# Third unit's values in one burst, first scores four matmuls later, another order of products in one step

## The chip, the cores and the metric

The kernel runs on one core of one Trainium2 chip. The metric is the time of one execution in device microseconds (us). Times in the text that look like 38.54 are positions in the profiled execution, counted from its first instruction.

## What is computed

Windowed causal attention with a window of 64 positions, and then a feed-forward block with a ReLU gate, on 4608 tokens:

```python
# attention: 8 batches, 8 heads, 576 positions, head dimension 64
scores = (q @ k.T) / sqrt(64); masked to 0 <= i - j < 64; softmax
x = (attn @ v)                 # transposed to (4608, 512)
# feed-forward: 512 -> 1536 -> 512
out = (maximum(x @ w_gate, 0) * (x @ w_val)) @ w_out
```

Inputs and output are float32; the kernel multiplies in float16 and adds up in float32.

## The kernel before

**Tiles and stages.** The tokens are taken in tiles `t`: 384, 192, 448 and then seven of 512. For a tile the attention is made (scores, exponential, mask, values, division, transposition to `xt`), then the gates (`hidden` and `fast_hidden`: both products, ReLU, multiplication into `g_sb`), then the output products with `w_out`. The attention of a later tile is woven into the gates and output products of an earlier one, so that TensorE (PE) always has something. The first two tiles are plain; their gates are matmuls of 192 columns (L634), their output products stand in L1145. From tile 2 on, the third, the gates use a scheme of seven products instead of eight (Strassen's kind): `fast_hidden` makes three steps `j` of products `P1` to `P7` for both weights.

**One step of the gates.** Each `P` is two groups of four matmuls (L740), one for the gate weight and one for the value weight. `TO` says into which of three PSUM banks per weight a product adds up: P1, P6, P7, P4 into `A`, P2 into `B`, P5 and P3 into `C`. `AFTER` says what a product waits for: P6 and P2 for the copy of A after P1 (L749), P7 for the copy of A after P6 (L759), P4 for the copy after P7 (L759), and P3 for the sum of P7's copy with C, which holds P5 (L776, made when both P5 and P7 have run). The result of P2 goes through a ReLU on ScalarE (L809) and a multiplication on VectorE (L765), which also frees its bank; P4's result goes the same way. The sums of P7 and P3 get a ReLU (L782) and are multiplied on GpSimd. After the last step of tile 2, `fast_output` (L874) first makes the scores of the next quad (L277) and then output products.

**Attention in quads and values.** `scores(qd, T, ...)` issues 64 small matmuls (48 for quad 1; L277, contraction over 32 rows) into four banks, and plans four exponentials on ScalarE (L450, L452) and four masks on VectorE (L459, L462). `values(t, hh, T, ...)` issues the products of probabilities and V for one half of the heads (L493, 32 columns wide, 56 matmuls for tile 2 and 64 for a tile of 512), and plans reciprocals (L507), normalisations (L515), the transposition or turn (L521) and, with `x_form` (L537), the differences of `xt` that the seven products need. `w_form` (L561) makes the sums and differences of the weights, `o_sign` (L894) negated copies of `w_out`, `v_spread` (L216) copies V within the core.

**What sets the order.** There is one list of due times, `W` (`Weaver`). `W.at(T, fn)` puts a piece of work down for the planned time `T`; the loops that issue PE's long products call `W.advance(W.clock)` ahead of each small group of matmuls, and whatever is due by the planned clock is issued there. A place in the program that needs a result pops the list until it is there. So the due times decide in which order the instructions of each engine stand; the engines then run their lists in order, with semaphores between them. Free PSUM banks come from one list, `free`, in the order in which they are given back.

The places of the change: L1279 puts down the scores of quad 0 (37.9), L1282 the values of the third unit, tile 2, for the two halves of the heads (45.0 and 45.7), and L849 the order of products in a step `j` of the gates where the scheme for the output is not the fast one (tiles 2 and 3).

Of the kernel before, what the change touches and what calls it, by code (L numbers as in the profile page):

```python
# [47 lines left out]
def kernel(  # L48
# [40 lines left out]
    singles = [psum.tile([128, 512], FP32, name=f"bank{i}") for i in range(8)]  # L89
# [19 lines left out]
    last = consts.tile([128, 2], FP16)  # L109
# [32 lines left out]
    W = Weaver()  # L142
# [52 lines left out]
    def qk_trans(b, name, hh, j0=0, j1=S // 32):  # L195

        src = nat[b, name, hh].bitcast(FP32).rearrange("p (j e) -> p j e", e=32)
        dst = qTs[b % 2][:, hh] if name == "q" else kTs[b % 2][:, hh, 64:64 + S]
        dst = dst.bitcast(FP32).rearrange("p c o -> p (c o)")
        nc.vector.transpose(dst.rearrange("p (i j) -> p j i", i=32)[:, j0:j1], src[:, j0:j1])  # L200
# [125 lines left out]
    def behind_quad(qd, g=G - 1):  # L326
        nc.gpsimd.tensor_copy(last[0:1], quads[qd]["p"][g][0:1, QW, 0:2])
# [105 lines left out]
    def q_st(qd, banks=None):  # L433

        d = quads[qd] = {"st": banks or [bank() for _ in range(G)], "p": [None] * G}
        unread.update(map(id, d["st"]))
        run_rows([[st_block(d["st"][g][:, 256 * hh + 64 * i:256 * hh + 64 * i + 64], g, hh, q_window(qd, i), False, hh + i > 0)
                   for hh in range(2) for i in q_wins(qd)] for g in range(G)])
        written.update((id(to), 512) for to in d["st"])
        return 0.72  # L440
# [4 lines left out]
    def q_exp(qd, g, give=True):  # L445
        d = quads[qd]
        d["p"][g] = a_p.tile([128, 2 * QW, 64], FP16, name="pw", tag="p")
        n = 64 * len(q_wins(qd))
        if n == 256:
            nc.scalar.activation(d["p"][g].rearrange("p n c -> p (n c)"), d["st"][g], ACT.Exp, scale=scale)  # L450
        else:
            nc.scalar.activation(q_part(qd, d["p"][g]), d["st"][g].rearrange("p (h n) -> p h n", h=2)[:, :, 0:n]  # L452
                                 .rearrange("p h (i c) -> p h i c", c=64), ACT.Exp, scale=scale)
        read(d["st"][g], give)

    def q_mask(qd, g):
        d = quads[qd]
        if len(q_wins(qd)) == QW:
            nc.vector.tensor_tensor(d["p"][g], d["p"][g], mask[:, None, :].to_broadcast([128, 2 * QW, 64]), MUL)  # L459
        else:  # L460
            p = q_part(qd, d["p"][g])
            nc.vector.tensor_tensor(p, p, mask[:, None, None, :].to_broadcast(p.shape), MUL)  # L462
        d["masked"] = d.get("masked", 0) + 1

    def scores(qd, T, banks=None, give=True):

        W.clock += q_st(qd, banks)
        for g in range(G):
            late = 0.8 if qd > 8 and qd % 2 and g == G - 1 else 0.0
            W.at(T + 0.8 + ((0.0, 0.3, 1.6, 1.9)[g] if qd == 7 else 0.6 * g + late), lambda g=g: q_exp(qd, g, give))  # L470
            W.at(T + 1.5 + 0.6 * g + late, lambda g=g: q_mask(qd, g))
# [72 lines left out]
    def values(t, hh, T, banks=None, give=False, turn=2.7):  # L544

        t_pv(t, hh, banks or [bank() for _ in range(3)], banks is None or give)
        W.clock += 0.62
        W.at(T + (1.15 if give else 0.7), lambda: t_recip(t, hh))
        for i, k in enumerate((2, 0, 1)[3 - len(banks or (0, 1, 2)):]):
            W.at(T + 1.2 + 0.5 * i, lambda k=k: t_norm(t, hh, k))  # L550
        W.at(T + turn, lambda: t_turn(t, hh))
        for n, x in (((0, 4.0),), ((1, 4.0), (2, 4.1), (3, 5.0)))[hh] if not give else ():
            W.at(T + x, lambda n=n: x_form(t, n))
# [146 lines left out]
    def fast_hidden(t, seven=None):  # L700
# [116 lines left out]
        def step(j, name):  # L817
            for i in range(2):
                product(j, name, i)
                if name == "P1":  # L820
                    seed(j, i)
                if name in ("P6", "P7"):
                    snap(j, name, i)
                if name == "P2":
                    direct(j, i, "B", 0)
                if name in ("P5", "P7") and (j, "ran", "P5", i) in at and (j, "ran", "P7", i) in at:
                    add(j, "P7", i, 1, 0.1 if name == "P5" else 0.8)
                if name == "P4":
                    direct(j, i, "A", 1)
                if name == "P3":  # L830
                    add(j, "P6", i, 0, 0.1)

        last = NF // 4 - 1
# [12 lines left out]
                    step(last, name)  # L846
            return
        for j in range(last + 1):
            for name in ("P5", "P6", "P2", "P7") if j == 0 else ("P6", "P2", "P7", "P5"):  # L849
                step(j, name)  # L850
            tail = [(j, "P4"), (j + 1, "P1"), (j, "P3")] if j else [(j + 1, "P1"), (j, "P4"), (j, "P3")]
            for jj, name in tail:
                if jj <= last:
                    step(jj, name)
# [342 lines left out]
    with tc.manual_schedule():  # L1197
# [78 lines left out]
        v_load(5, ((NG - 1, 64, 128),))  # L1276
        for i, (name, hh) in enumerate((n, hh) for n in "kq" for hh in range(2)):
            W.at((31.4, 31.6, 33.2, 34.3)[i], lambda name=name, hh=hh: qk_trans(1, name, hh))
        W.at(37.9, lambda: scores(0, 37.9, singles[4:8], False))  # L1279
        W.at(41.2, lambda: scores(1, 41.2, singles[4:8], False))  # L1280
        W.at(44.6, lambda: behind_quad(1))
        for hh, T in enumerate((45.0, 45.7)):  # L1282
            W.at(T, lambda hh=hh, T=T: values(2, hh, T, singles[4 + 2 * hh:6 + 2 * hh], True, 1.75))
        for n, T in enumerate((46.8, 49.2, 49.3, 49.4)):
            W.at(T, lambda n=n: x_form(2, n))
# [67 lines left out]
        def begin(t):  # L1353
            if t not in running:
                running[t] = fast_hidden(t, sevens.get(t))
                next(running[t])
# [82 lines left out]
```

## Time and profile before

| | |
|---|---|
| median of three runs | 299.24 us (298.9 to 299.25) |
| the profiled execution | 299.36 us, of which its span 297.7 us |
| granted TensorE clock | 1.000 |
| PE busy | 287.8 us, 97% of the span |
| VectorE (DVE) busy | 255.6 us, 86% |
| ScalarE (ACT) busy | 203.2 us, 68% |
| GpSimd (POOL) busy | 190.1 us, 64% |

The span runs from the first to the last instruction of the core; the rest of the profiled execution's time lies around it. Busy PE time counts overlapping matmuls, whose ends are modelled, so the time between the starts of two matmuls says more than a matmul's length. A row of the timeline gives the start in us, the length in us, engine, line, operation, output and inputs, and how many instructions were merged; in brackets stands the idle time of the engine before it and what ended it. A row of the chain gives start, length and what was running.

### The profile page before, as it was taken

To read this page: it belongs to the slowest core of one execution; us is meant where nothing else is said; L and a number is where in the kernel's file an instruction comes from. 1 tells how busy PE (TensorE), PEld (TensorE's weight loads), DVE (VectorE), ACT (ScalarE), POOL (GpSimd) and SP (SyncE) were. 2 spreads that over 40 slices of the span, in tenths; PEclk is the share of its full clock that TensorE was granted. 3 is DMA by queue.
4 is the path that set the end of the run, shared out by engine and by line. 5 is a ranking of instruction groups with operands and counts; after the bars stand their busy time and mean duration, and the time that the engine had idled before them with its cause. 6 is when DMAs were issued, how large, how long until landed. Compare 5 with 4: busy or idle time off the path is not lost.

```text
span 297.7 us, 11066 instructions
## 1 busy us (share of the span) xinstructions
PE 287.8 (97%) x4659; PEld 241.7 (81%) x4659; DVE 255.6 (86%) x513; ACT 203.2 (68%) x409; POOL 190.1 (64%) x217
## 2 busy tenths in 40 slices
PE   4799999999999999999999999999999999999995
PEld 2489976996588756898888888888888888888894
DVE  5978989797889799899999999989858985896585
ACT  3744367888378848974898479857985698637850
POOL 8767667897927637485948595759375617441751
PEclk9999999999999999999999999999999999999999
DMA  7999999977998779911499239912911210021013
GB/s 219 183 197 196 195 194 200 244 94 127 168 208 161 109 131 195 205 37 37 77 216 115 54 63 219 125 53 57 175 34 34 78 37 0 3 90 55 1 39 106
DMA packets 62610, 35.22 MB, mean 118 GB/s; under 512 B 39648, under 2 KB 56672, under 8 KB 62560
## 3 DMA queue, kind: packets, MB, share of 16 engines
q0 software_dynamic: 49376, 20.26, 57.5%
q1 hardware_dynamic: 12752, 13.93, 15.2%
q8 instruction: 36, 0.59, 0.8%
q10 hardware_dynamic: 432, 0.33, 0.3%
q14 instruction: 14, 0.11, 0.1%
HBM read 37.75 MB, written 9.44 MB: 159 GB/s over the span
## 4 chain that ended last, share of the span: by engine, by line
PE 94%; DVE 3%; DMA 1%; issue 0%; ACT 0%; DVEq 0%
PE bank L740 49%; PE bank L966 19%; PE bank L874 7%; PE bank L634 6%; PE bank L1145 4%; PE bank L277 4%; PE bank L493 3%; PE bank L672 1%; DMA vs<-in_k_dram 1%; DVE qT L200 1%; DVE kT L200 1%; PE bank L348 1%; PE bank L667 0%; DVE nats L193 0%; PE bank L241 0%
## 5 line engine op out<-in xcount | busy, mean ns | idle before, releaser
L765 POOL TENSOR_TENSOR g_sb<-pr 128x512 f16<-128x512 f32 (+1 forms) x36 | 46.2, 1286 | 51.3 <-ACT pr L782 47.7
L776 DVE TENSOR_TENSOR pr<-bank,pr 128x512 f32<-128x512 f32 (+1 forms) x96 | 60.7, 672 | 3.0 <-PE bank L740 1.5
L759 ACT COPY pr<-bank 128x512 f32<-128x512 f32 (+1 forms) x96 | 51.1, 589 | 14.0 <-PE bank L740 13.9
L765 DVE TENSOR_TENSOR g_sb<-r,bank 128x512 f16<-128x512 f32 (+1 forms) x48 | 32.4, 676 | 22.6 <-ACT r L809 20.9
L966 PEld LDWEIGHTS <-g_sb 128*128 128x128 f16 x444 | 41.8, 98 | 5.0
L740 PE MATMUL bank<-xc,us 128*128 128x256 f16 (+2 forms) x292 | 42.7, 269 | 0.0
L740 PE MATMUL bank<-xc,vs 128*128 128x256 f16 (+2 forms) x292 | 42.7, 269 | 0.0
L740 PEld LDWEIGHTS <-vs 128*128 128x128 f16 x392 | 37.7, 98 | 3.9
L740 PEld LDWEIGHTS <-us 128*128 128x128 f16 x392 | 37.6, 98 | 3.9 <-issue 0.2
L206 POOL DMA_DIRECT2D v<-in_v_dram x41 | 36.8, 1117 | 5.8 <-DMA wo<-in_moe_w_out_dram 2.5
L782 ACT ACTIVATE pr<-pr 128x512 f32<-128x512 f32 (+1 forms) x48 | 30.3, 632 | 8.4 <-DVE pr L776 8.4
L450 ACT ACTIVATE pw<-bank 128x512 f16<-128x512 f32 x60 | 32.0, 606 | 2.4 <-PE bank L277 2.1
L809 ACT ACTIVATE r<-bank 128x512 f32<-128x512 f32 (+1 forms) x48 | 28.8, 600 | 5.4 <-PE bank L740 4.7
L740 PEld LDWEIGHTS <-wg 128*128 128x128 f16 x300 | 28.4, 98 | 3.1
L740 PEld LDWEIGHTS <-wv 128*128 128x128 f16 x300 | 28.4, 98 | 2.7
L740 PE MATMUL bank<-xt,wg 128*128 128x256 f16 (+2 forms) x200 | 28.5, 267 | 0.0
L740 PE MATMUL bank<-xt,wv 128*128 128x256 f16 (+2 forms) x200 | 28.5, 267 | 0.0
L916 POOL TENSOR_TENSOR g_sb<-g_sb,xus 128x512 f16<-128x512 f16 x24 | 27.0, 1145 | 0.0
L966 PE MATMUL bank<-wo,g_sb 128*128 128x256 f16 (+1 forms) x222 | 26.6, 270 | 0.0
L749 ACT COPY bank<-bank 128x512 f32<-128x512 f32 (+1 forms) x48 | 25.6, 577 | 0.0
L966 PE MATMUL bank<-wts,g_sb 128*128 128x256 f16 (+1 forms) x222 | 25.6, 270 | 0.0
L459 DVE TENSOR_TENSOR pw<-pw,mask 128x512 f16<-128x512 f16 x60 | 23.1, 427 | 2.1 <-ACT pw L450 1.7
(125 smaller groups left out, 519.7 us busy)
## 6 DMA issues: line engine op xcount, KB each, us to landing
out_dram<-o_sb SPq DMA_DIRECT2D x31, 256.0 KB, 3.8
nats<-in_k_dram POOLq DMA_DIRECT2D x15, 288.0 KB, 6.0
nats<-in_q_dram POOLq DMA_DIRECT2D x15, 288.0 KB, 6.9
v<-in_v_dram POOLq DMA_DIRECT2D x31, 128.0 KB, 9.1
v<-v SPq DMA_DIRECT2D x12, 132.0 KB, 3.5
v<-v SPq DMA_DIRECT2D x24, 66.0 KB, 3.0
wg<-in_moe_w_gate_dram POOLq DMA_DIRECT2D x6, 256.0 KB, 7.5
wv<-in_moe_w_val_dram POOLq DMA_DIRECT2D x6, 256.0 KB, 8.7
```

Of the source, the lines that this page charges most:

```text
L206: nc.gpsimd.dma_start(v16s[b % 2][lo:hi, g, :, 0:64], v[b, :, 64 * g - 64 + lo:64 * g - 64 + hi].rearrange("h p d -> p h d"))
L450: nc.scalar.activation(d["p"][g].rearrange("p n c -> p (n c)"), d["st"][g], ACT.Exp, scale=scale)
L459: nc.vector.tensor_tensor(d["p"][g], d["p"][g], mask[:, None, :].to_broadcast([128, 2 * QW, 64]), MUL)
L740: nc.tensor.matmul(to[:, HT * m + lo:HT * m + lo + step], w[:, k, 128 * m:128 * m + 128], x[:, k, lo:lo + step], start=(first and m == 0 a ...
L749: nc.scalar.copy(at[j, "B", i][:, 0:TW], at[j, "A", i][:, 0:TW])
L759: nc.scalar.copy(pr[:, i], at[j, "A", i][:, 0:TW])
L765: eng.tensor_tensor(gh[:, f:f + 2, h], pair(r), pair(v), MUL)
L776: nc.vector.tensor_tensor(pr[:, i], to[:, 0:TW], pr[:, i], ADD)
L782: nc.scalar.activation(pr[:, 0], pr[:, 0], ACT.Relu)
L809: nc.scalar.activation(r, to[:, 0:TW], ACT.Relu)
L916: eng.tensor_tensor(to, x, y, op)
L966: nc.tensor.matmul(at[key][:, QN * m * whole:QN * m * whole + n1 - n0], A[:, 128 * m:128 * m + 128], B[:, c, n0:n1] if len(B.shape) == 3 e ...
```

## The change

Three edits. The scores of quad 0 are due at 38.4 instead of 37.9. The second half of the third unit's values is due at 45.05 instead of 45.7, 0.05 after the first half. In the last step of tile 2's gates (`j == last and t == 2`) the products run in the order P6, P5, P7, P2 instead of P6, P2, P7, P5.

```diff
         for j in range(last + 1):
-            for name in ("P5", "P6", "P2", "P7") if j == 0 else ("P6", "P2", "P7", "P5"):
+            for name in ("P5", "P6", "P2", "P7") if j == 0 else ("P6", "P5", "P7", "P2") if j == last and t == 2 else ("P6", "P2", "P7", "P5"):
                 step(j, name)
...
-        W.at(37.9, lambda: scores(0, 37.9, singles[4:8], False))
+        W.at(38.4, lambda: scores(0, 38.4, singles[4:8], False))
         W.at(41.2, lambda: scores(1, 41.2, singles[4:8], False))
         W.at(44.6, lambda: behind_quad(1))
-        for hh, T in enumerate((45.0, 45.7)):
+        for hh, T in enumerate((45.0, 45.05)):
             W.at(T, lambda hh=hh, T=T: values(2, hh, T, singles[4 + 2 * hh:6 + 2 * hh], True, 1.75))
```

In the built program this moves, on PE, four matmuls of the gates from behind the 64 scores of quad 0 to ahead of them, and four output products from between the two halves of the third unit's values to behind them; on ScalarE one ReLU (L605) ahead of quad 0's first exponential, and in tile 2's last step the two copies of P7 ahead of the ReLU of P2; on VectorE the first masks of quad 0 behind one more gate multiplication, the reciprocals and two of the normalisations of the third unit ahead of its first turn, and the two sums of P7 ahead of the multiplication of P2. Two PSUM banks change places from there to the end. Count and kind of instructions are the same, and the lists of GpSimd and of the SP queue are unchanged.

## The prediction

> **What bounds the kernel now.** I read the page first: the engines' busy shares and the chain that ended last.
>
> ```profile
> span 297.7 us, 11066 instructions
> ...
> PE 287.8 (97%) x4659; PEld 241.7 (81%) x4659; DVE 255.6 (86%) x513; ACT 203.2 (68%) x409; POOL 190.1 (64%) x217
> ...
> PE 94%; DVE 3%; DMA 1%; issue 0%; ACT 0%; DVEq 0%
> ```
>
> TensorE (PE) is busy for 97% of the span and 94% of the chain is its own work. So a microsecond that PE does not lose is a microsecond of the run, unless another engine then makes it wait. The list of PE's waits, longest first, shows what there is to win:
>
> ```profile
> PE bank L244 <- DVE bias L130: 4.4, 1, 4.4
> ```
>
> This is the start of the kernel; the others in the list are 0.7 us or less and lie before 15.1 us, where the change does nothing. What it can save must be short stalls that this list does not count. Those I looked for in the chain in order of time (start, length, what).
>
> ```profile
> 27.01 10.68 PE bank L634 x128
> ...
> 38.54 0.67 PE bank L277 x63
> ...
> 43.08 3.78 PE bank L1145 x18
> 46.85 0.55 PE bank L493 x50
> 47.41 0.76 PE bank L1145 x4
> 48.16 0.60 PE bank L493 x48
> 48.76 4.89 PE bank L1145 x36
> ...
> 107.97 0.88 PE bank L493 x87
> ...
> 108.89 0.43 PE bank L493 x32
> ...
> 137.35 1.27 PE bank L493 x124
> ...
> 228.36 1.18 PE bank L493 x118
> ...
> 257.32 0.62 PE bank L493 x53
> ...
> 261.12 0.62 PE bank L493 x60
> ```
>
> One sees the two places of the first two edits: the scores at 38.5 us (L277), and the values (L493) in two bursts with four output products (L1145) between them. L634 gives the pace of a 192-wide matmul, 10.68/128 = 0.083 us.
>
> **Edit one: the first quad's scores asked for at 38.4 instead of 37.9.** In the built order of PE the four matmuls of the next gate tile (the first half of its eight) now stand ahead of the 64 score matmuls instead of behind them; nothing else moves on PE here. The timeline around it:
>
> ```profile
> 38.27 0.94 PE L277 MATMUL bank<-qT,kT 32*128 32x64 f16 x64
> ...
> 39.26 0.60 ACT L450 ACTIVATE pw<-bank 128x512 f16<-128x512 f32 x1 [0.34 <-PE bank L277]
> ...
> 40.02 0.49 ACT L605 ACTIVATE pr<-bank 128x384 f32<-128x384 f32 x1 [0.15 <-PE bank L634]
> 40.40 1.57 ACT L450 ACTIVATE pw<-bank 128x512 f16<-128x512 f32 x3
> ...
> 41.21 0.42 DVE L459 TENSOR_TENSOR pw<-pw,mask 128x512 f16<-128x512 f16 x1
> ...
> 42.53 0.55 PE L277 MATMUL bank<-qT,kT 32*128 32x64 f16 x48
> ...
> 44.73 1.17 DVE L462 TENSOR_TENSOR pw<-pw,mask 128x384 f16<-128x384 f16 x4
> 45.81 0.42 DVE L561 TENSOR_TENSOR us<-wg 128x512 f16<-128x512 f16 x1
> ...
> 46.78 0.51 PEld L493 LDWEIGHTS <-pw 128*32 128x32 f16 x56 [0.42 <-issue]
> ...
> 48.82 1.11 DVE L521 STREAM_TRANSPOSE xt<-xw 128x896 f16<-128x896 f16 x1
> ...
> 50.64 1.15 DVE L515 TENSOR_TENSOR xw<-bank,rw 128x448 f16<-128x448 f32 x2
> ```
>
> The scores start at 38.27, but in the chain the second of them starts only at 38.54: it needed a bank that VectorE (DVE) was still multiplying out of (L614). The same 64 matmuls take 0.68 at 69.75 (row below), so the wait costs 0.94 - 0.68 = 0.26 us. Four matmuls ahead of it take 4 x 0.083 = 0.33, so the scores start at 38.60, after 38.54: the wait goes whole, **0.26 us**.
>
> What comes late for it is on ScalarE (ACT). There the relu of that gate tile (L605) moves ahead of the first exponential. Its product is finished 0.26 earlier, so the relu starts at 40.02 - 0.26 = 39.76; an exponential follows a relu after 0.38 (40.40 - 40.02); the three take 1.57, so with 0.60 for one they follow each other at (1.57 - 0.60)/2 = 0.48. The four start from 40.14 and end at 40.14 + 3 x 0.48 + 0.60 = 42.18, where they ended at 41.97. The next scores need their banks at 42.53 - 0.26 = 42.27. The cover is 0.09 us; gone, each 0.1 us costs 0.1 (a rival below). On DVE one mask more (0.42) stands behind the last gate, whose input is 0.26 earlier: what follows is late by at most 0.16, the second quad's masks end by 45.90 + 0.16 = 46.06, and the values need them at 46.78 - 0.26 = 46.52. The order of GpSimd (POOL) and of the SP queue does not change, and no DMA is moved.
>
> **Edit two: the third unit's values in one burst.** The four output products go behind the second burst, in PE's built order; count and operands stay. The row of weight loads shows why a burst costs more than its matmuls: before it PE's weight loading idles 0.42 us with nothing to wait for. The four products between the bursts took 0.76; two are 512 and two 256 wide, three times a 512 one, and 18 of these took 3.78, so they are worth 3 x 0.21 = 0.63: 0.13 goes. The bursts of 56 took 0.55 + 0.60 = 1.15; the one burst of 128 at 137.35 took 1.27, which for 112 is 1.11: 0.04 more. Sum **0.17 us**. Bounds: the burst at 228.36 (1.18) gives 1.03 for 112 and a gain of 0.25; the two halves of 64 at 257.32 and 261.12 took 1.24 together, 0.03 less than 1.27, and a gain of 0.10. I take 0.17, since 1.27 is the nearest in size and the commonest.
>
> What this moves on DVE: two reciprocals, and of the four normalisations (half of 1.15 each) one, come ahead of the first turn (L521), whose end was 48.82 + 1.11 = 49.93. With 0.58 for the one, some 0.3 for reciprocals and 0.16 from above it ends by 51.0. PE has output products until 48.76 + 4.89 = 53.65, now 53.22, and only then needs that turn: 2.2 us of cover. The work of both halves is the same, and the second half's input comes earlier, so the second turn and the differences behind it are no later.
>
> **Edit three: last step of the third tile's gates.** P6, P2, P7, P5 becomes P6, P5, P7, P2; P4 and P3 follow as before. Each name is two groups of four matmuls.
>
> ```profile
> 64.83 0.61 DVE L765 TENSOR_TENSOR g_sb<-r,bank 128x448 f16<-128x448 f32 x1
> ...
> 66.91 0.55 PE L740 MATMUL bank<-xc,vs 128*128 128x224 f16 x4
> ...
> 67.38 0.98 ACT L759 COPY pr<-bank 128x448 f32<-128x448 f32 x2
> ...
> 68.07 1.15 DVE L776 TENSOR_TENSOR pr<-bank,pr 128x448 f32<-128x448 f32 x2
> ...
> 68.82 0.55 PE L740 MATMUL bank<-xt,us 128*128 128x224 f16 x4
> ...
> 69.28 0.54 PE L740 MATMUL bank<-xt,vs 128*128 128x224 f16 x4
> ...
> 69.75 0.68 PE L277 MATMUL bank<-qT,kT 32*128 32x64 f16 x64
> ```
>
> Groups follow each other at 0.38 to 0.39 (their four at 224/256 of the wide ones); from 68.82 to 69.28 it is 0.46. P3's second group waits for the sum of P7 with P5 (L776), which ends at 68.07 + 1.15 = 69.22. That is **0.07 us**. In the new order (times of this trace) P7's second group, still at 66.91, ends at 67.46; the relu that stood ahead of the two copies of P7 (L759) now follows them, so the second copy starts at about 67.5 and ends by 68.1; the second sum then ends near 68.85 instead of 69.22, and P3's second group can start at 69.20 unhindered. P4's two groups, 0.77 and 0.38 ahead of 68.82, need the copies no later than before and have them by 67.7 and 68.1. P5 now starts three groups ahead of 66.91, at 65.76, and needs the banks that L765 at 64.83 frees by 65.44. Late is now P2: its multiplication frees a bank that the scores at 69.68 want, and it stands behind both sums, from about 68.8 to 69.4. Cover 0.25.
>
> **The sum.** 0.26 + 0.17 + 0.07 = 0.50 us. The profiled execution took 299.36 (span 297.7, the rest around it untouched): 298.86. The median of the three runs, 299.24, lies 0.12 below it: **298.74**. Its own range, by the bounds of edit two and a lost margin in edit one, is 0.36 to 0.58, 298.66 to 298.88. About 0.2%, 0.60 us, is what a measurement of this kernel can tell from no change: the three runs lie between 298.9 and 299.25.
>
> **Rivals.** *The long burst runs dry* (0.09). The burst at 107.97 halted after 87 matmuls and took 0.88 + 0.43 and the pause, to 109.32: 1.35, with no releaser named, 0.17 more than the shortest.
>
> ```profile
> q8 instruction: 36, 0.59, 0.8%
> ```
>
> If that was a supply of instructions that ran out (36 packets for PE's 9318, about 259 each, at 0.8% of 16 engines' span over 36 = 1.06 us each), a burst of 112 with 224 instructions in 1.1 us can meet it, where two bursts with a rest between them cannot. It would take the 0.17 of edit two: 299.03 profiled, 298.91. Against it: 137.35 passed 128 without a halt. The Trainium skill, "Runtime: NRT & Kernel Launch", section Instruction fetch mechanics, says that instructions come in blocks of 16 KiB, 256 instructions, loaded while the current one executes, so that the crossing is mostly hidden; that block size agrees with the row, and of the hiding one burst of these in six or so looks otherwise.
>
> *The exponentials are late* (0.07). The cover of 0.09 fails because one exponential more than I count stands in front; price at most the 0.26 won: total 0.24, 299.00.
>
> *More than the sum* (0.18). The halt at 108.9, which no wait in the list explains, is a matter of timing and does not return: up to 0.50 + 0.17 = 0.67, 298.57.
>
> *Slower* (0.10). One mechanism: the second quad's masks on DVE (L462). Due times set DVE's order; if the masks miss the start of the burst because DVE's sums for the weights (L561, four at 0.42, 1.68) come between, the values start 1.68 - 0.46 = 1.22 late, and so does all behind them: -0.50 + 1.22 = +0.72, 299.96. It decides at 46.52. Against it: the built order has the masks ahead of the sums. A wait of this size in a part that I hold covered stands here too.
>
> That the edits do nothing is excluded: PE's order shows all three.
>
> **How the numbers follow.** The forecast has 0.56. It lies 0.10 us short of the bound while the runs scatter over 0.35, so I let 4 in 10 of it, 0.22, read as faster by over 0.2%; with 0.16 of the bigger gain's 0.18 that is 0.38. Within 0.2% fall the rest of the forecast, 0.34, the dry burst, 0.09, the late exponentials, 0.07, and 0.02 of the bigger gain: 0.52. Slower has 0.10. The range 298.4 to 299.2 holds all but the slower case and the tails: it ends 0.2 beyond the late exponentials and the dry burst, and 0.17 below the bigger gain, for the scatter.
>
> **What would show it.** Right: 64 scores near 38.6 in one run of 0.68; one values row of 112 near 46.5, and the tile's first gate product near 53.1; no 0.46 step before the third tile's last group; everything after 70 us earlier by 0.5 with the same steps. Wrong: a PE gap before the second scores at 42.3, a halt within the new burst, or scores at 69.2 that start late.

## The result, and the profile after

The changed kernel took 298.63 us in the median (298.47 to 299.29, 22 runs), the kernel before 299.10 (298.87 to 299.35, 22 runs, in the same comparison): 0.47 us less. The ratio on record is 0.9987 with a 95% interval of 0.9981 to 0.9993, which is 0.2 to 0.6 us less; the quotient of the two medians alone would be 0.9984. The prediction had 0.50 us less than before, and 298.74, counted from a median of three runs that was itself 0.14 above the median of 22.

The profiled execution of the changed kernel took 298.50 us, with a span of 296.8 at a granted clock of 0.999. That is 0.86 less than the 299.36 of before, so 0.39 more than the medians differ; a part of this is chance, as the chain of waits shows (start, length, what):

```profile
26.73 11.66 PE bank L634 x140
...
46.31 1.11 PE bank L493 x105
47.42 5.54 PE bank L1145 x40
52.96 16.10 PE bank L740 x168
...
107.21 1.26 PE bank L493 x117
...
256.46 0.62 PE bank L493 x57
```

The reader is to see four things against the rows of before. The gate products that start the stretch stand at 26.73 where they stood at 27.01: 0.28 us earlier, before any edit has acted. All 140 products of 0.083 run through to the scores, which start at 38.32 (in the timeline below) and are not held up. One row of values stands at 46.31 where there were two with a row of four output products between. And the burst at 107 runs through, where that of before halted at 108.85 and took 1.35 (107.97 to 109.32) instead of 1.26.

So the start is taken out by measuring from the first row of that stretch (27.01 of before, 26.73 here) to the start of the values at 257, past every place that the change touches: 257.32 - 27.01 = 230.31 before, 256.46 - 26.73 = 229.73 after. The difference is 0.58, of which 0.09 is the halt. What is left is 0.49. Below this distance is called the stretch.

The same places in the timeline of the changed kernel:

```profile
38.32 0.68 PE L277 MATMUL bank<-qT,kT 32*128 32x64 f16 x64
...
39.86 2.06 ACT L450 ACTIVATE pw<-bank 128x512 f16<-128x512 f32 x4
...
41.98 0.55 PE L277 MATMUL bank<-qT,kT 32*128 32x64 f16 x48
...
44.42 1.16 DVE L462 TENSOR_TENSOR pw<-pw,mask 128x384 f16<-128x384 f16 x4
...
46.24 1.18 PE L493 MATMUL bank<-v,pw 128*32 128x65 f16 x112
...
49.41 1.11 DVE L521 STREAM_TRANSPOSE xt<-xw 128x896 f16<-128x896 f16 x1
...
52.80 0.55 PE L740 MATMUL bank<-xt,wg 128*128 128x224 f16 x4
...
67.04 1.16 DVE L776 TENSOR_TENSOR pr<-bank,pr 128x448 f32<-128x448 f32 x2 [1.22 <-ACT pr L759]
...
68.13 0.55 PE L740 MATMUL bank<-xt,us 128*128 128x224 f16 x4
...
68.52 0.55 PE L740 MATMUL bank<-xt,vs 128*128 128x224 f16 x4
```

The 64 scores now take the 0.68 of an undisturbed block. The four exponentials end at 39.86 + 2.06 = 41.92 and the second block of scores starts at 41.98: a cover of 0.06 us is left. The sums of P7 with P5 end at 67.04 + 1.16 = 68.20, ahead of P3's second group, which now follows its first by 0.39 (68.13, 68.52), no longer by 0.46.

### The profile page after: what moved, and what is told of

Read it like the earlier page. It is cut to its first block, busy times and chain, and to the rows that moved or that the text cites. A ratio compares the mean times of both kernels' runs of the same rounds, so it can differ in the third digit from the quotient of the medians.

```text
span 296.8 us, 11064 instructions
## 1 busy us (share of the span) xinstructions
PE 287.5 (97%) x4659; PEld 242.0 (82%) x4659; DVE 254.8 (86%) x513; ACT 203.4 (69%) x409; POOL 190.4 (64%) x217
## 4 chain that ended last, share of the span: by engine, by line
PE 94%; DVE 3%; DMA 1%; ACT 0%; issue 0%; DVEq 0%
PE bank L740 49%; PE bank L966 19%; PE bank L874 7%; PE bank L634 6%; PE bank L277 4%; PE bank L1145 4%; PE bank L493 3%; DMA vs<-in_k_dram 1%; PE bank L672 1%; DVE qT L200 1%; DVE kT L200 1%; PE bank L348 1%; PE bank L667 0%; PE bank L241 0%; ACT nats L193 0%; DVE pr L1133 0%
## 5 line engine op out<-in xcount | busy, mean ns | idle before, releaser
L765 POOL TENSOR_TENSOR g_sb<-pr 128x512 f16<-128x512 f32 (+1 forms) x36 | 46.3, 1289 | 51.0 <-ACT pr L782 47.5
L759 ACT COPY pr<-bank 128x512 f32<-128x512 f32 (+1 forms) x96 | 51.1, 588 | 14.0 <-PE bank L740 13.8
L765 DVE TENSOR_TENSOR g_sb<-r,bank 128x512 f16<-128x512 f32 (+1 forms) x48 | 32.4, 676 | 21.4 <-ACT r L809 19.3
L809 ACT ACTIVATE r<-bank 128x512 f32<-128x512 f32 (+1 forms) x48 | 28.8, 600 | 5.2 <-PE bank L740 4.3
```

The source lines that it names most:

```text
L759: nc.scalar.copy(pr[:, i], at[j, "A", i][:, 0:TW])
L765: eng.tensor_tensor(gh[:, f:f + 2, h], pair(r), pair(v), MUL)
L809: nc.scalar.activation(r, to[:, 0:TW], ACT.Relu)
```

## The experiments

All times are medians; the ratio stands against the kernel before on the same chip.

### The kernel before once more

> The kernel before, unchanged, profiled once more. If the halts at 17.05 and 108.89 of its first trace belong to its order of instructions, they stand in this trace again, at the same matmuls; if they are chance, they are gone or elsewhere. Ratio 1.0000; what the interval misses of that shows how fine the comparison is.

Measured: 299.13 us, ratio 0.9999 (0.9990 to 1.0008). The row of its chain that answers to the halt at 108.9, and the two ends of the stretch:

```profile
27.01 10.68 PE bank L634 x128
...
107.98 1.26 PE bank L493 x121
...
257.24 0.62 PE bank L493 x54
```

The halt at 17, which the trace of before has at 17.05, stands here again at 17.03, ahead of the same matmul; the one at 108.9 is gone, and the burst took 1.26. So the burst's halt comes and goes in one and the same program: the place is fixed, and whether it halts is chance. The stretch is 230.23. This is the base for all that follows; a kernel whose burst at 107 halts has what it lost there taken off.

### Edit one alone

```diff
-        W.at(37.9, lambda: scores(0, 37.9, singles[4:8], False))
+        W.at(38.4, lambda: scores(0, 38.4, singles[4:8], False))
```

> The kernel before with edit one alone (the first quad's scores four products later). Theory: the wait of the second score matmul on the multiplication of L614 goes whole, 0.26 us; the 64 scores start near 38.6 on the clock of the trace of before and take the 0.49 us of the other blocks of 64 from their first to their last start, where before they took 0.75; the second block of scores is not held up, since in the trace after its last bank came free 0.06 us ahead of it. Time 0.26 below the kernel before, ratio 0.9991. Rival, the exponentials are late: the scores gain, and the second block gives back up to all of it; ratio 1.0000.

Measured: 298.83 us, ratio 0.9991 (0.9982 to 1.0000). In its chain:

```profile
26.74 11.66 PE bank L634 x140
...
256.69 0.62 PE bank L493 x57
```

The stretch is 229.95, 0.28 less than the base, with no gap ahead of the scores and none at the second block. The wait on L614 went whole, and the exponentials were not late.

### Edit two alone

```diff
-        for hh, T in enumerate((45.0, 45.7)):
+        for hh, T in enumerate((45.0, 45.05)):
```

> The kernel before with edit two alone (the third unit's values in one burst). Theory as on record: 0.17 us less, bounds 0.10 to 0.25; by the trace after it is 0.13 to 0.14, since from the last product ahead to the first behind the burst of 112 costs 1.21 beyond the time of products where the two of 56 cost 0.65 and 0.69. Ratio 0.9995. Rival, the long burst runs dry: a halt of 0.2 inside the burst of 112, ratio 1.0000. Whether the burst at 108 halts here tells if that halt belongs to the order of instructions (then it comes wherever the count ahead of it is the same, as here) or to chance.

Measured: 298.84 us, ratio 0.9991 (0.9982 to 1.0000). The chain:

```profile
26.78 10.68 PE bank L634 x128
...
42.85 3.78 PE bank L1145 x18
46.63 1.11 PE bank L493 x105
...
53.28 16.17 PE bank L740 x168
...
107.60 0.88 PE bank L493 x87
...
108.57 0.43 PE bank L493 x30
...
256.99 0.62 PE bank L493 x57
```

From the output products at 42.85 to the first gate products it is 53.28 - 42.85 = 10.43, before it was 53.65 - 43.08 = 10.57: 0.14 won. The new burst runs through in 1.11, the figure that the prediction had worked out for it. The halt in the burst at 107 is in its old place again and costs 0.14 (108.57 + 0.43 - 107.60 = 1.40 against 1.26), although the burst before it is another. The stretch is 230.21, or 230.07 without that halt: 0.16 below the base.

### Edit three alone

```diff
-            for name in ("P5", "P6", "P2", "P7") if j == 0 else ("P6", "P2", "P7", "P5"):
+            for name in ("P5", "P6", "P2", "P7") if j == 0 else ("P6", "P5", "P7", "P2") if j == last and t == 2 else ("P6", "P2", "P7", "P5"):
```

> The kernel before with edit three alone (P6, P5, P7, P2 in the last step of the third tile). Theory: the step of 0.46 ahead of P3's second group becomes 0.38, everything behind it is 0.07 us earlier; ratio 0.9998, which the times alone cannot tell from 1, so the trace is what decides. Rival: the late multiplication of P2 holds up the scores at 69.2, and nothing is won.

Measured: 299.10 us, ratio 1.0000 (0.9991 to 1.0009), which decides nothing, as expected. The chain does:

```profile
26.70 10.68 PE bank L634 x128
...
53.34 16.10 PE bank L740 x168
69.44 0.62 PE bank L277 x64
...
256.86 0.62 PE bank L493 x56
```

The 168 products of the third tile take 16.10, as in the changed kernel, where edit two alone had 16.17: 0.07 won, and the scores behind them start without a gap. The stretch is 230.16, 0.07 below the base. The three edits alone give 0.28 + 0.16 + 0.07 = 0.51; together they gave 230.23 - 229.73 = 0.50. They add up, and no one of them takes anything from another. The medians are too coarse for this sum: the three edits alone lie 0.33, 0.32 and 0.06 below the 299.16 of the kernel before in that comparison.

### Scores later still

```diff
-        W.at(38.4, lambda: scores(0, 38.4, singles[4:8], False))
+        W.at(38.9, lambda: scores(0, 38.9, singles[4:8], False))
```

> The changed kernel with the first quad's scores asked for at 38.9 instead of 38.4, which puts eight more products of 0.083 us ahead of them. Theory: edit one has used its cover up to 0.06 us, which is what the trace after leaves between the last exponential and the second block of scores. The exponentials come later by the relus and products put ahead, 0.33 to 0.66, so the second block waits 0.27 to 0.60 and the time rises by that against the changed kernel: it is 0.2 below to 0.15 above the kernel before. Rival: the exponentials have more room than that, since their order on ScalarE moves too; then it is as fast as the changed kernel, ratio to before 0.9985.

Measured: 298.93 us, ratio 1.0000 (0.9982 to 1.0019); the interval is wide because one of the eleven executions took 301.88. The chain:

```profile
27.05 10.68 PE bank L634 x128
...
38.87 0.21 DVE g_sb L614
...
39.12 0.49 PE bank L634 x4
...
257.00 0.62 PE bank L493 x54
```

and one row of the timeline:

```profile
43.17 0.60 ACT L450 ACTIVATE pw<-bank 128x512 f16<-128x512 f32 x1 [1.32 <-PE bank L277]
```

The stretch is 229.95: 0.22 of the gain is lost again. The size lies just below what the theory gave, but its place is wrong. The wait is not at the second block of scores. Of the eight products moved in addition the first four run on without a gap; it is the last four (L634 at 39.12) that wait, once more for a bank that VectorE frees with the next L614. VectorE's pairs of multiplications of that part, L613 and L614, start 0.53 apart here (L613 at 37.93, 38.45 and 38.98), and what PE puts too early waits for the end of a pair: the scores in the trace of before, the products here. So the change has hit a small window: the four products that it puts ahead of the scores fit, twelve do not. Eight were not run.

The run has a second fault, and it bounds the due time more sharply. The fourth exponential of a quad is due 0.8 + 3 x 0.6 = 2.6 behind the quad's scores, here at 41.5. The scores of quad 1 are due at 41.2 and are given the same four banks (`singles[4:8]`). So the fourth exponential now stands behind the second block of scores, as the row above shows: it runs at 43.17, the block at 42.54. It reads a bank that this block has already written into, and this kernel therefore leaves out the true scores of one group of quad 0. Its time tells where PE waits; it is not a kernel to be used. In the changed kernel the fourth exponential is due at 38.4 + 2.6 = 41.0, only 0.2 ahead of that edge. For the same reason the run does not test whether the exponentials are late: the second block waited for three of them and not for four.

### A burst cut in another place

```diff
-            between = [[score(0)], [score(1)], [value(0), value(1)], []]
+            between = [[score(0)], [score(1)], [value(0)], [value(1)]] if t == 2 else [[score(0)], [score(1)], [value(0), value(1)], []]
```

> The changed kernel with the fourth unit's values, one burst of 128 at 75.6, cut into two bursts of 64 with twelve output products between them: edit two undone in another place. Theory (a burst has a price for going in and out, beside its matmuls): two halves at the 0.716 of those at 257 and 261 cost 1.43, the whole 1.34: 0.09 us slower than the changed kernel, and no halt. By the price of edit two, 0.135 for one going in and out, it is 0.14 slower. Rival (the price of a burst grows faster than its length, as its matmuls are 8.8 ns apart in the long ones and 7.7 in those of 64): the cut costs nothing or gains. The second half comes later for VectorE's turns; if these are late for the next tile, a wait shows at its first products.

Measured: 298.76 us, ratio 0.9988 (0.9979 to 0.9997). The chain:

```profile
26.68 11.66 PE bank L634 x140
...
75.64 0.62 PE bank L493 x54
...
78.96 0.69 PE bank L493 x63
...
82.34 18.34 PE bank L740 x168
...
107.33 0.88 PE bank L493 x87
...
108.36 0.43 PE bank L493 x30
...
256.78 0.62 PE bank L493 x57
```

The two halves and 24 output products took 82.34 - 75.64 = 6.70. In the changed kernel the whole burst and the same 24 took 6.53, from 75.69 to the gate products at 82.22:

```profile
75.69 1.25 PE bank L493 x121
...
82.22 18.34 PE bank L740 x168
```

So 0.17 more for one more way in and out of a burst, with no wait at the next tile. The halt at 108.2 cost 1.46 - 1.26 = 0.20 here (107.33 to 108.36 + 0.43 = 108.79). Without it the stretch is 230.10 - 0.20 = 229.90, 0.17 above the changed kernel. The rival falls; the price is somewhat over the expected 0.09 to 0.14, and edit two's 0.14 to 0.16 is the same thing seen from the other side. The ratio, 0.9988 against 0.9987 for the changed kernel in another comparison, is too coarse to show it.

### The masks behind the sums

```diff
-                                  ... (45.55, 0.0, nc.vector, sums[0][4:8]),
+                                  ... (44.5, 0.0, nc.vector, sums[0][4:8]),
```

> The changed kernel with VectorE's four sums for the weights (L561) due at 44.5 instead of 45.55, which puts them ahead of the last of the second quad's four masks (L462): the slower rival made true for one mask. Theory: in the trace after the last mask is done at 45.60 and the first weight load that needs it is at 46.49, a cover of 0.89; the four sums put ahead take about 1.55, so the load waits 0.6 and the kernel is 0.6 slower than the changed one, 0.2 slower than before, ratio 1.0007. Rival: what waits is a later part of the burst, and less than 0.3 is lost.

Measured: 299.19 us, ratio 1.0004 (0.9995 to 1.0013). The timeline:

```profile
47.08 0.74 PEld L493 LDWEIGHTS <-pw 128*32 128x32 f16 x77 [0.61 <-DVE pw L462]
```

and the ends of its stretch in the chain:

```profile
26.62 11.66 PE bank L634 x140
...
115.00 0.73 PE bank L277 x62
...
257.08 0.62 PE bank L493 x57
```

The weight loads of the burst idle 0.61 for the last mask, and the block at 115.00 is 0.12 longer than the 0.61 that this block took in the changed kernel. Without these 0.12 the stretch is 230.46 - 0.12 = 230.34, which is 0.61 above the changed kernel: the 0.6 of the theory. So the slower rival was a real mechanism with the price that the rows gave for one mask. In the changed kernel the masks end at 44.42 + 1.16 = 45.58, 0.66 ahead of the burst, and it does not act.

### One more order, and one more due time

The trace before and the trace after both show a stall that the change left alone: in the first step of the fifth tile's gates P7 waits for copies on ScalarE (L759). The timeline of the changed kernel:

```profile
117.10 1.11 ACT L450 ACTIVATE pw<-bank 128x512 f16<-128x512 f32 x2
...
118.07 1.11 ACT L759 COPY pr<-bank 128x512 f32<-128x512 f32 x2
118.12 0.60 PE L740 MATMUL bank<-xt,wv 128*128 128x256 f16 x4
118.73 0.60 PE L740 MATMUL bank<-xc,us 128*128 128x256 f16 x4
```

P7's first group (118.73) starts 0.61 behind the one ahead of it instead of 0.44, since the copies stand behind two exponentials of the scores at 114.4 in ScalarE's order. Two ways were tried. First, other work ahead of P7:

```diff
-            for name in ("P5", "P6", "P2", "P7"):
-                step(0, name)
-            for j, name in ((1, "P1"), (0, "P4"), (0, "P3"), ...
+            for j, name in ((0, "P5"), (0, "P6"), (0, "P2")) + (((1, "P1"), (0, "P7")) if t == 4 else ((0, "P7"), (1, "P1"))):
+                step(j, name)
+            for j, name in ((0, "P4"), (0, "P3"), ...
```

> The changed kernel with one more reorder of the same kind: in the first step of the fifth tile's gates (t is 4) the first products of the next step (P1) go ahead of P7, which in both traces waits 0.18 and 0.06 us for ScalarE's copies (L759) that stand behind two exponentials. Theory: P7 comes 0.87 later, the copies are done by then, 0.23 less than the changed kernel, ratio to before 0.9979. Rival: P1 then asks for banks that are not free at 118.7 and waits instead, or its own copy on ScalarE (L749) pushes the copies that P4 needs; then nothing is won.

Measured: 300.76 us, ratio 1.0052 (1.0038 to 1.0065), slower. The list of PE's waits:

```profile
PE bank L740 <- DVE pr L776: 0.9, 1, 0.9
...
PE bank L740 <- ACT r L809: 0.6, 1, 0.6
PE bank L740 <- ACT pr L759: 0.4, 1, 0.4
```

The columns are the time in total, the number of waits and the longest. The rival holds, and more: P1's second group waits for the bank that the ReLU of P2 still reads (L809), then P4 for the copies of P7, which ScalarE now makes after the seed copies of P1, then P3 for the sum. Three waits of 1.9 in all by this list, for one of 0.23; the stretch, 258.74 - 26.84 = 231.90, is 2.17 above the changed kernel.

Second, PE's order kept, and on ScalarE the fourth exponential (which is not wanted before the values at 136) behind the copies instead of ahead:

```diff
-            W.at(T + 0.8 + ((0.0, 0.3, 1.6, 1.9)[g] if qd == 7 else 0.6 * g + late), lambda g=g: q_exp(qd, g, give))
-            W.at(T + 1.5 + 0.6 * g + late, lambda g=g: q_mask(qd, g))
+            W.at(T + 0.8 + ((0.0, 0.3, 1.6, 3.2)[g] if qd == 7 else 0.6 * g + late), lambda g=g: q_exp(qd, g, give))
+            W.at(T + 1.5 + ((0.0, 0.6, 1.7, 3.3)[g] if qd == 7 else 0.6 * g + late), lambda g=g: q_mask(qd, g))
```

> The changed kernel with the fourth exponential (L450) of the scores at 114.4 asked for 1.3 later on ScalarE, and the last two masks of these scores 0.1 behind their exponentials; PE's sequence of products stays, the banks have other numbers. It then stands behind the copies of P6 (L759) that P7 waits for at 118.74 and 119.23 and behind the relu of P2. Theory: the first of these copies starts 0.47 earlier, P7's two waits of 0.18 and 0.06 go, and the kernel is 0.23 faster than the changed one (ratio to before 0.9979). Rival: the bank of the late exponential, or the copies of P7 behind it, are wanted at 119.9 or 120.4, and a new wait there takes the 0.23 or more.

Measured: 298.26 us (298.18 to 298.58), ratio 0.9973 (0.9963 to 0.9984). The timeline:

```profile
117.49 1.10 ACT L759 COPY pr<-bank 128x512 f32<-128x512 f32 x2
...
118.46 0.60 PE L740 MATMUL bank<-xc,us 128*128 128x256 f16 x4
...
118.92 0.66 ACT L450 ACTIVATE pw<-bank 128x512 f16<-128x512 f32 x1
```

The copies stand at 117.49 instead of 118.07, with the exponential behind them, and P7 starts at 118.46 without a wait. The stretch, from 26.62 to 256.13 in its chain, is 229.51, 0.22 below the changed kernel. With 4.0 in place of 3.2 (and 4.1 for its mask) the exponential stands between the two copies of P7:

> As the run before, with that exponential another 0.8 later, between the two copies of P7. Theory: the same 0.23, as P4 has the second copy by 120.65 and asks for it at 120.81. Rival: the second copy and the seeds behind it (L749) are too late, and up to 0.3 of a wait comes at P4 or at the next step's P6.

Measured: 298.55 us, ratio 0.9982 (0.9973 to 0.9992); the stretch, 256.23 - 26.61 = 229.62, is only 0.11 below the changed kernel.

P7's waits are gone here too, but P1's second group starts 0.08 late (119.86 instead of 119.78 in the run before): it waits for VectorE's multiplication of P2 (L765), which ends at 119.12 + 0.69 = 119.81, and half the gain is lost. The median does not show even the other half, as it is not below the changed kernel's 298.51; the lowest executions, 298.18, 298.27 and 298.39 for the run before, this one and the changed kernel, stand in the order of the stretches. The changed kernel in the same comparison:

> The changed kernel once more, in the same comparison as the two runs before: ratio to before 0.9985, and in its trace the waits at 118.7 again and no halt in the burst of 112. Whether the burst at 107.1 halts after 95 matmuls is chance (it did in 3 of 10 traces of all kernels so far), and costs 0.10 to 0.20 where it does.

Measured: 298.51 us, ratio 0.9983 (0.9974 to 0.9991), stretch 256.68 - 26.93 = 229.75, where the first trace had 229.73, with no halt in either burst.

So one exponential at 3.2 makes a kernel 0.25 us faster than the changed one (298.26 against 298.51 on one chip; 0.22 and 0.24 in the stretch), and 0.77 faster than the one before (299.03 there).

## Why the prediction was right, by its steps

**Edit one, 0.26.** Held: 0.28 alone in the stretch, and the row of 64 scores went from 0.94 to 0.68. The relu and the exponentials moved as worked out: on a clock that runs 0.28 ahead they were to end at 42.18 - 0.28 = 41.90 and ended at 41.92, and the cover was 0.06 where 0.09 had been worked out. What the prediction did not see is that the window has another edge close by: the later scores lost 0.22, not by the exponentials that it watched but by VectorE's next multiplication. Nor did it see that the due time itself has an edge, 0.2 further on, behind which the fourth exponential reads the wrong scores.

**Edit two, 0.17.** The mechanism held, the size is 0.14 in the rows and 0.16 alone, inside its bounds. The term that was a little large is the products' part. The burst itself took the 1.11 that was set for it, 0.04 less than the two. The output products around it took 3.78 (in edit two's run, as before) and 5.54, 9.32 together, where 3.78 + 0.76 + 4.89 = 9.43 stood: 0.11, not 0.13.

**Edit three, 0.07.** Held: 16.17 to 16.10. The late multiplication of P2 left the scores behind it alone (53.34 + 16.10 = 69.44, where they start in that run).

**The cover on VectorE.** Both held: the first turn ended at 49.41 + 1.11 = 50.52, 2.28 ahead of the first gate product at 52.80 (2.2 was said), and the masks were ahead of the burst by 0.66, where at least 0.46 was said.

**The sum.** 0.50 was forecast; the stretch gives 0.50 against the base, the medians 0.47. The terms missed by 0.02 one way (edit one) and by 0.01 to 0.03 the other (edit two), so that the sum comes out to the hundredth is luck. For the profiled execution 298.86 was forecast and 298.50 came; the 0.36 between them is, but for rounding, the 0.28 of the start and the 0.09 of the halt, which no edit made.

**The rivals.** That the exponentials are late did not happen; the cover held at 0.06, and no run tested what its loss costs. That the masks fall behind the sums did not happen, and costs 0.6 for one mask where it is made to happen. The other two rested on the halt at 108.9, and there the prediction had each half right and drew the wrong line between them. It is a matter of timing, as the bigger gain had it, but it has not gone with the change: it stands in 3 of 13 traces, those of the kernel before, of edit two alone and of the cut burst. So it belongs to the scatter and not to the difference, which is why the profiled executions differ by more than the medians. And a long burst can halt, as the dry burst had it, but the burst of 112 did so in none of nine traces.

## What to carry to other kernels

Where one engine is busy for 97%, a change of a few tenths can be forecast from the rows of the chain: count what a row takes beyond the same row elsewhere, and then look for who is next on every bank that comes free. The stalls that are left are windows with two edges; a due time that is right at 38.4 is wrong at 38.9, and the second edge is one of meaning, not of time: where two blocks share banks, ask of each new due time whether the first block is still read ahead of the second's writing. Ahead of moving the bound engine's own order, look at what the waiting engine has in front of the awaited piece: one exponential put behind two copies gave 0.25 us, while moving products ahead of the wait cost 2.17 in the stretch.

## What the runs showed of the hardware

**Halts at fixed places, by chance.** Counted in order over all 4659 matmuls of each trace, from zero, the halts of PE that no wait explains come ahead of matmul 223 (the 17.05 of before; 3 of 13 traces), 1758 (the 108.9; 3 of 13, at 0.09, 0.14 and 0.20 us) and 1886 (at 115.1 in the run with late masks, 0.12; 1 of 13). The distances are 1535 and 128 matmuls. Each has a weight load, and two semaphore instructions stand in the first stretch: 3072 and 256 instructions, 12 times and once 256. The Trainium skill, "Runtime: NRT & Kernel Launch", section Instruction fetch mechanics, says that instructions are refilled in blocks of 256 and that a crossing is mostly hidden. The places agree with that block size, and "mostly" is here some crossings that show in a quarter of the traces or less. In the burst of 112, the crossing falls on its 17th matmul (1758 less 8 x 128 is 734, one more for the two semaphore instructions, which stand behind it, and the burst begins with 719), and none of nine traces halted there. That the refill is the cause was not shown: no run changed it, only the places speak for it. Against a supply that simply ran out, as the prediction had it, stand the packets of the queue q8 in the traces: at each of the seven halts the last one had landed 1.1 us or more ahead (by 107.42 for the halt that begins at 108.65 in the trace of before), and none was under way.

**A burst of small matmuls has a price for its ends.** One cut more cost 0.17 us with 64 matmuls a side, one fewer gave 0.14 to 0.16 with 56, although the matmuls follow each other faster in the two bursts of 56 (7.8 and 8.6 ns from start to start) than in the one of 112 (8.9 ns).
